# Chunk 0's first half: U by substitution over 32-token blocks in place of a 64-token inverse, and two query masks at an earlier place

## The chip, the cores and the metric

The kernel runs on 1 core of one Trainium2 chip. The time is device microseconds of one execution. Engines are called PE (TensorE), DVE (VectorE), ACT (ScalarE), POOL (GpSimd) and SP (SyncE, which here issues DMAs).

## The reference

```python
# batch B=4, heads H=8, sequence S=768, head size D=48
k_n = k / (norm(k) + 1e-6)
for t in range(S):
    y[:, :, t] = q[:, :, t] @ state
    v_old = state^T k_n[:, :, t]
    state = state + beta_t * outer(k_n[:, :, t], v_t - v_old)
x = y.transpose(0, 2, 1, 3).reshape(B * S, H * D)      # 3072 x 384
h = x @ w_in                                           # 384 -> 2048
out = (h * sigmoid(h)) @ w_out                         # 2048 -> 384
```

A recurrence over tokens (a delta rule) for each batch and head, followed by a feed-forward block over all tokens.

## The kernel before

The 768 tokens are cut into 6 chunks of 128, and each chunk into two halves of 64 (`hf`). The four batches form two groups `g` of two. In one half the update vectors U of all tokens follow from a triangular system: U = X (V - K S), with S the state at the start of the half and X the inverse of a 64x64 triangular matrix that is made of the score blocks (`aps[c, g][0]`), the key norms and beta. Chunk 0 begins with a zero state, so in its first half no term of the state enters.

For chunk 0, the scores are stored to memory and fetched back as blocks (`block_out`, `block_in`), `invert_first` inverts 16-token corners on DVE by rank-one steps, and then PE joins them in stages: `corner` and `straight` make the inverses of the four 32-token diagonal blocks of the partitions (into `xi`), `turned` makes a transposed copy of the even blocks, and `merge_half` (a first and a second product) fills in the 32x32 block between them, so that `xi` holds the 64-token inverse. Each stage is a generator over 16 heads-and-batches of one group `g`; it ends with copies out of PSUM by ACT and DVE. `joins(hf)` strings these stages together; between them single steps of the weights' narrowing are written in by hand (`fill`, `begin_next`). `narrow` takes a piece of 768 words per partition through two steps on ACT (L233, L234), two on DVE (L238, L242) and one on POOL (L246).

After the joins `masks` (L1364) multiplies the query scores of chunk 0 by a triangle, `solve(0)` runs `inner` (U = X V, L840; U goes to `zbuf` for the state and, for this first half, to `slab` for the outputs) and `first_outputs` (L884), which makes the transposed outputs `xT` of the first half; its last step is an add on DVE (L893). Then the first `hidden` product (L1046) can begin. The second half's joins (`joins(1)`) are laid between the first hidden products by the long script string: in it `s` is one step of `solve`, `f` one of `fill`, `q` the turning of one batch's queries, `j` one step of `joins(1)`, `b` is `begin_next`, `r` half a hidden product.

The order on each engine is written out: `pin` chains every operation behind the one before it on its engine. DMAs on SP's queue are in one line too. The later weight loads are paced: each is issued when a running count of PE's work (4 for a matmul, 2 for a transpose) reaches a number in `loads`. PSUM banks are handed out in turn from three rooms, `A` (3 banks), `CC` (3) and `M` (2). A matmul in fp32 appears as two PE instructions in the trace.

Of the kernel before, what the change touches and what calls it, by code (L numbers as in the profile page):

```python
# [13 lines left out]
ALU = mybir.AluOpType  # L14
# [5 lines left out]
def kernel(  # L20
# [10 lines left out]
    nc = tc.nc  # L31
    B, H, S, D = q.shape
    DM, DFF = moe_w_in.shape
    P = 128
# [5 lines left out]
    W = 64  # L40
# [622 lines left out]
    def invert_first(step):  # L663
# [77 lines left out]
        def straight(g, hf):  # L741

            pls = [bank(room, "pl") for room in (A, CC)]
            for i, n, k in heads(g, hf):
                for j in (2 * k + 1, 2 * k):
                    pin(nc.tensor.matmul(
                        pls[k][rows[j], T * i : T * (i + 1)], lhsT=y[rows[j], n, :],
                        rhs=up[rows[j], n, :], start=True, stop=True,
                    ))
                    yield  # L750
            for odd in (1, 0):
                for k, by in enumerate((by_act, by_dve)):
# [68 lines left out]
    def by_heads(t):  # L821
        return t[:, 0:DM].rearrange("p (u a d) -> p u a d", u=HB, a=NP)
# [12 lines left out]
    def inner(c, g, hf, room=CC):  # L835

        pz = bank(room, "pz")
        for u, p, e, n, _, _ in of_heads():
            rows = on(e, hf, g)
            yield pin(nc.tensor.matmul(  # L840
                pz[rows, n * D : (n + 1) * D], lhsT=xis[g][rows, u * H + 2 * p + e, :],
                rhs=vfs[c][rows, hf, g * HB + u, p, :], start=True, stop=True,
            ))
        to = zbuf[:, g * HB : (g + 1) * HB, hf, :, 0:D]
        if c == 0 and hf == 0:
            by = (by_act, by_dve) if g == 0 else (by_dve, by_act)
            at = slab[:, g * HB * NP * 2 * D + D :][:, 0 : HB * NP * 2 * D]
            by[0](at.rearrange("p (n w) -> p n w", w=2 * D)[:, :, 0:D], pz[:, 0:DM].rearrange("p (n d) -> p n d", d=D))
            by[1](to, by_heads(pz))
        else:  # L850
            by_act(to, by_heads(pz))

    def update(c, g, hf):

# [123 lines left out]
    def solve(c):  # L978

        if c == 0:  # L980
            together(inner(0, 0, 0, CC))
            together(inner(0, 1, 0, M))
            yield
            first_outputs(0)
            yield
            first_outputs(1)
            yield
            together(update(0, 0, 0), update(0, 1, 0))
            yield
# [12 lines left out]
            yield  # L1002
            return
        together(merge(c, 0, False), merge(c, 1, False))
        yield
        together(keys(c, 0, 0), keys(c, 1, 0))
        yield
        together(merge(c, 0, True), merge(c, 1, True))
        yield
        for hf in range(2):  # L1010
            if hf == 1:
                together(keys(c, 0, 1), keys(c, 1, 1))
                if c > 1:
# [12 lines left out]
            if hf == 0:  # L1026
                yield
# [286 lines left out]
    def first_queries(b):  # L1314
# [3 lines left out]

        score(0, b, (1,), (A, CC), evacuate)

    for b in range(2):
        turn(0, b, 1, M, b == 0)
    block_in(0)
# [18 lines left out]
    for b in range(2, B):  # L1342
# [19 lines left out]
    def masks(g, u):  # L1362
        to = aps[0, g][1][:, u]
        pin(nc.vector.tensor_tensor(  # L1364
            out=to, in0=to, in1=above[:].unsqueeze(1).to_broadcast([P, H, W]), op=ALU.mult
        ))

    for n in range(1 + Q):
        done = next(inv)
# [12 lines left out]
    pin(nc.gpsimd.memset(slab, 0.0))  # L1382

    def joins(hf, between=()):

        for stage in (
            corner(0, hf), corner(1, hf), turned(0, hf), turned(1, hf), straight(0, hf), merge_half(0, hf, False),
            straight(1, hf), merge_half(1, hf, False), merge_half(0, hf, True), merge_half(1, hf, True),
        ):
            yield from stage  # L1390
            for what in between[:1]:
                what()
            between = between[1:]

    def filled(n):
        return lambda: fill(n)

    def sized():
        size_half(0, pins[seen_on])
        begin_next()  # L1400

    def none():
        pass

    together(joins(0, [
        lambda: (size_half(0, pins[seen_on]), begin_next(),),
        lambda: (),
        lambda: (),
        lambda: (fill(1), fill(1),),
        lambda: (fill(1),),  # L1410
        lambda: (),
        lambda: (fill(1),),
        lambda: (fill(1), begin_next(),),
        lambda: (),
        lambda: (),
    ]))
    masks(0, 0)
    masks(0, 1)
    masks(1, 0)
    masks(1, 1)  # L1420

    pieces = chained(hidden(0, 0), hidden(0, 1), project())

# [146 lines left out]
                pieces = chained(feed_forward(1, 0), feed_forward(1, 1))  # L1570

    for text in (
        "s f3 s q q s j32 b j20 r f j8 q f j4 f j16 r j44 b j4 q j4 r f r j22 f j12 f j8 f b j8 f j4 r j20 e r f j99 h f r f2 l s l r l p r l f p l s l2 f r3 l3 p l s l4 p l2 s r l f l4 f l f l2 p l s l2 s p f r f r l r l2 g i p l p f i p f l i r2 i r v f i3 r3 i r i r i3 b r2 f2 r2 i r2 i2 r2 i f b i r i3 f2 r2 f r3 f i2 r f i f r3 f r f i f i2 r i r i k i2 b z r2 i r i r z r i r2 b r t s r b r f s r2 t s m r m t2 r b m f t m s f b r m2 b m f s r m r s m4 s m3 c m4 s r t G m r2 m4 V m s r m r m t2",
    ):
        script(text)
    for c in range(1, NCH):
# [62 lines left out]
```

## Time and profile before

| | us |
|---|---|
| timed runs, median (lowest to highest of 3) | 639.25 (639.19 to 642.03) |
| span of the profiled execution, first to last instruction | 636.1 |
| PE busy in it | 622.4 |
| DVE busy | 397.5 |
| ACT busy | 214.3 |
| first hidden product starts | 52.46 after the span's start |

For the profiled execution only the span is given; its own time, with what lies around the span, isn't. The median of the timed runs is 3.15 above the span. Times in the profile are microseconds from the first instruction. A row of the chain gives start, length and what ran; "issue" is time in which an engine waited for nothing that the profile shows. A row of stretches gives busy time and number of instructions of PE, weight loads, DVE, ACT and POOL, then the clock granted to PE (1.00 is full speed), the busy share of the DMA engines and GB/s. A row of a group gives line, engine, operation, output<-input, shapes and number, then busy time and mean ns of one, then the idle time before.

### The profile page before, as it was taken

How to read it: one execution, taken by the hardware profiler on the slowest of the kernel's cores; microseconds unless marked ns; L12 is line 12 of the kernel's file. 1: busy time of each engine (PE TensorE's matmuls, PEld its weight loads, DVE VectorE, ACT ScalarE, POOL GpSimd, SP SyncE). 2: the span in 40 equal slices, each digit the busy share in tenths (PEclk: the TensorE clock that was granted, in tenths of full speed). 3: DMA queues.
4: the chain of work that ended last, by engine and by line, in shares of the span. 5: the costliest groups of instructions: out<-in, count | busy, mean ns of one | idle time of the engine just before them, and what ended most of it. 6: DMA issues, size and time to landing. Idle time of an engine off the chain costs nothing.

```text
span 636.1 us, 21387 instructions
## 1 busy us (share of the span) xinstructions
PE 622.4 (98%) x9406; PEld 547.3 (86%) x9406; DVE 397.5 (62%) x910; ACT 214.3 (34%) x500; POOL 89.9 (14%) x92
## 2 busy tenths in 40 slices
PE   7979999999999999999999999999999999999997
PEld 5568788656799989989989989989989989989997
DVE  5786879999677974546974555975455964112112
ACT  3456673423351122451122451122451122441120
POOL 5033721345020020020020010020002000000000
PEclk9779999999999999999999999999999999999999
DMA  7966726350458460459151359232253133010101
GB/s 114 227 159 177 218 67 148 100 99 4 95 105 174 72 104 8 94 107 183 37 91 21 75 124 164 56 84 29 64 117 76 26 75 37 16 38 1 26 0 26
DMA packets 145676, 54.70 MB, mean 86 GB/s; under 512 B 117152, under 2 KB 138912, under 8 KB 145584
## 3 DMA queue, kind: packets, MB, share of 16 engines
q1 hardware_dynamic: 143136, 52.93, 40.5%
q8 instruction: 74, 1.21, 0.8%
q10 hardware_dynamic: 2448, 0.41, 0.4%
q14 instruction: 18, 0.15, 0.1%
HBM read 40.14 MB, written 11.01 MB: 80 GB/s over the span
## 4 chain that ended last, share of the span: by engine, by line
PE 94%; DVE 2%; DMA 1%; issue 1%; ACTq 0%; ACT 0%; POOL 0%; SPq 0%; DVEq 0%; POOLq 0%
PE phid L1046 40%; PE px L1163 17%; PE py L1163 13%; PE po L1090 5%; PE pb_c L840 3%; PE pa L529 2%; PE pb_c L828 2%; PE pyc L919 2%; PE pb_c L1090 2%; PE pb_c L860 2%; PE pyc L906 1%; PE px L782 1%; PE py L782 1%; PE pt L500 1%; DMA sums_of_w<-blocks 1%
## 5 line engine op out<-in xcount | busy, mean ns | idle before, releaser
L1046 PE MATMUL phid<-xT,w_in 128*128 128x256 f32 x1152 | 257.0, 381 | 0.2 <-DVE xT L893 0.2
L1046 PEld LDWEIGHTS phid<-xT,w_in 128*128 128x128 f32 x1152 | 216.4, 190 | 30.2 <-issue 0.9
L1056 ACT ACTIVATE gT<-phid 128x512 f32<-128x512 f32 x88 | 52.5, 597 | 144.8 <-PE phid L1046 140.5
L1144 DVE TENSOR_TENSOR sums_of_g<-gT 128x384 f32<-128x384 f32 (+1 forms) x60 | 30.4, 529 | 65.7 <-ACT gT L1056 55.4
L627 DVE SCALAR_TENSOR_TENSOR rank<-g,step,x 128x31 f32<-128x31 f32 (+15 forms) x124 | 49.8, 401 | 21.7 <-DMA g<-blocks 18.1
L1163 PE MATMUL px<-sums_of_w,sums_of_g 128*128 128x192 f32 x320 | 56.6, 329 | 0.0
L1163 PE MATMUL py<-w_out,sums_of_g 128*128 128x192 f32 x320 | 56.2, 328 | 0.0
L1163 PEld LDWEIGHTS py<-w_out,sums_of_g 128*128 128x128 f32 x320 | 52.3, 190 | 0.3
L1163 PEld LDWEIGHTS px<-sums_of_w,sums_of_g 128*128 128x128 f32 x320 | 52.2, 190 | 0.4
L632 DVE TENSOR_TENSOR x<-x,rank 128x31 f32<-128x31 f32 (+15 forms) x124 | 42.5, 342 | 4.3
L467 POOL TENSOR_TENSOR vf<-vf,n_slot 128x768 f32<-128x768 f32 x10 | 14.8, 1494 | 174.4 <-DMA vf<-in_v_dram 150.4
L544 ACT COPY xT<-pyc 48x128 f32<-48x128 f32 (+2 forms) x126 | 32.7, 260 | 1.7
L488 DVE STREAM_TRANSPOSE kq<-stage 128x512 f32<-128x512 f32 x28 | 28.4, 1115 | 5.2 <-DMA stage<-in_q_dram 5.2
L1163 PE MATMUL py<-w_out,gT 128*128 128x192 f32 x160 | 28.9, 330 | 0.0
L1174 DVE TENSOR_TENSOR o<-o,kept 128x192 f32<-128x192 f32 (+1 forms) x29 | 11.5, 422 | 26.7 <-ACT kept L1171 26.7
L1163 PE MATMUL px<-w_out,gT 128*128 128x192 f32 x160 | 27.9, 327 | 0.0
L1163 PE MATMUL px<-sums_of_w,gT 128*128 128x192 f32 x160 | 27.8, 327 | 0.0
L1163 PEld LDWEIGHTS px<-w_out,gT 128*128 128x128 f32 x160 | 26.5, 190 | 0.6
L550 POOL COPY g<-x 64x256 f32<-64x256 f32 x4 | 5.0, 1242 | 151.9 <-DVE x L635 151.9
L1163 PEld LDWEIGHTS py<-w_out,gT 128*128 128x128 f32 x160 | 26.1, 190 | 0.4
L865 DVE TENSOR_TENSOR state<-state,pb_c 128x384 f32<-128x384 f32 x22 | 11.2, 550 | 24.1 <-PE pb_c L860 24.1
L1163 PEld LDWEIGHTS px<-sums_of_w,gT 128*128 128x128 f32 x160 | 26.2, 190 | 0.1
(222 smaller groups left out, 931.2 us busy)
## 6 DMA issues: line engine op xcount, KB each, us to landing
vf<-in_v_dram SPq DMA_DIRECT2D x48, 96.0 KB, 2.8
out_dram<-o SPq DMA_DIRECT2D x42, 96.0 KB, 2.2
w_out<-in_moe_w_in_dram SPq DMA_DIRECT2D x4, 768.0 KB, 4.7
sums_of_w<-in_moe_w_out_dram SPq DMA_DIRECT2D x4, 768.0 KB, 4.1
blocks<-ap SPq DMA_DIRECT2D x44, 64.0 KB, 1.9
g<-blocks SPq DMA_DIRECT2D x5, 512.0 KB, 3.5
kb<-in_k_dram SPq DMA_DIRECT2D x12, 192.0 KB, 4.2
kb<-in_k_dram SPq DMA_DIRECT2D x24, 96.0 KB, 4.3
```

Source lines behind the costliest of these rows:

```text
L467: pin(nc.gpsimd.tensor_tensor(out=vf, in0=vf, in1=of, op=ALU.mult))
L488: pin(nc.vector.transpose(out=kqs[c, b][:, :, j, :].rearrange("p a (i m) -> p a m i", i=T), in_=src.rearrange("p a (m d) -> p a m d", d=D) ...
L529: pin(nc.tensor.matmul(pa[e][half, p * n * W : (p + 1) * n * W], lhsT=kq[rows, p, 0, half], rhs=kq[rows, p, js[0] : js[-1] + 1, half], sta ...
L544: return pin(nc.scalar.copy(to, of))
L627: pin(nc.vector.scalar_tensor_tensor(out=tv, in0=g[:, 0:m, m : m + 1].to_broadcast([P, m, n]), scalar=step[:, m : m + 1], in1=x[:, m : m + ...
L632: yield pin(nc.vector.tensor_tensor(out=x[:, 0:m, m:T], in0=x[:, 0:m, m:T], in1=tv, op=ALU.add))
L840: yield pin(nc.tensor.matmul(pz[rows, n * D : (n + 1) * D], lhsT=xis[g][rows, u * H + 2 * p + e, :], rhs=vfs[c][rows, hf, g * HB + u, p, : ...
L1046: pin(nc.tensor.matmul(ph[:, j * GT : (j + 1) * GT], lhsT=w_in[:, a, (2 * f + j) * P : (2 * f + j + 1) * P], rhs=xTs[c, hf][:, a, :], star ...
L1056: pin(nc.scalar.activation(out=hidden_of(c, hf, f), in_=ph[:], func=ACTF.Silu, scale=-0.5 if in_blocks(c) else 0.5))
L1090: pin(nc.tensor.matmul(pos[i][:, 0:DM], lhsT=hidden_of(0, hf, f // 2)[:, at : at + C], rhs=w_outs[f // HFF][:, f % HFF, :], start=(f == 0) ...
L1144: pin(nc.vector.tensor_tensor(out=sums_of_g[:, k, fs], in0=of[0], in1=of[1], op=op))
L1163: pin(nc.tensor.matmul(to, lhsT=at, rhs=quarter(f, *b) if isinstance(b, tuple) else sums_of_w[b][:, f], start=start and f == 0, stop=f == ...
```

## The change

For chunk 0's first half the 64-token inverse is no longer made. After `corner` and `straight`, `first_block` multiplies the even 32-token diagonal inverse with the values (U of the first 32 tokens), `across` multiplies the score block between the two with this U and adds it to the values of the odd block, and `last_block` multiplies the odd diagonal inverse with these. `turned`, both merges and `inner` are gone for this half; the second half of chunk 0 and all later chunks are as before. `last_block`'s result is copied to `slab` by ACT and, by `keep_last`, to `zbuf` by DVE. `straight` copies even blocks first in this half.

The scaling of the values (`size_half(0, ...)`, POOL) moves ahead of the clearing of `slab` (POOL). The masks of group 0 move to just behind that group's query scores, before the inversion; the masks of group 1 stand behind `across(1)`. Of the eight narrowing steps between `corner` and the second half's joins, five now come behind `first_outputs(1)` (`f5` in the script), where before three stood between `inner` and `first_outputs(0)` and none behind `first_outputs(1)`. Two paced loads (`fetch_w_out` 3 and 4) have numbers that are 128 lower, as much as the count falls short by the removed matmuls; the other numbers stay.

```diff
-            for odd in (1, 0):
+            for odd in ((0, 1) if hf == 0 else (1, 0)):
...
+    def first_block(g):
+        pz = both_blocks[g] = bank((CC, M)[g], "pz")
+        for u, p, e, n, _, _ in of_heads():
+            even, _ = blocks_of(e ^ g)
+            yield pin(nc.tensor.matmul(
+                pz[even, n * D : (n + 1) * D], lhsT=xis[g][even, u * H + 2 * p + e, 0:T],
+                rhs=vfs[0][even, 0, g * HB + u, p, :], start=True, stop=True,
+            ))
+        for k, by in enumerate((by_act, (by_dve, by_act)[g])):
+            even, _ = blocks_of(k)
+            by(zbuf[even, g * HB : (g + 1) * HB, 0, :, 0:D], by_heads(pz)[even])
+    def across(g):
+        pr = bank(CC, "pr")
+        ...
+                pr[odd, n * D : (n + 1) * D], lhsT=aps[0, g][0][even, u, 2 * p + e, T:W],
+                rhs=zbuf[even, g * HB + u, 0, p, 0:D], start=True, stop=True,
+        ...
+            pin(nc.vector.tensor_tensor(out=to, in0=to, in1=by_heads(pr)[odd], op=ALU.add))
+    def last_block(g):
+        ...
+                pz[odd, n * D : (n + 1) * D], lhsT=xis[g][odd, u * H + 2 * p + e, T:W],
+                rhs=vfs[0][odd, 0, g * HB + u, p, :], start=True, stop=True,
+        ...
+        by_act(at.rearrange("p (n w) -> p n w", w=2 * D)[:, :, 0:D], pz[:, 0:DM].rearrange("p (n d) -> p n d", d=D))
...
         if c == 0:
-            together(inner(0, 0, 0, CC))
-            together(inner(0, 1, 0, M))
-            yield
             first_outputs(0)
...
     first_queries(1)
+    masks(0, 0)
+    masks(0, 1)
     step = block_steps(0)
...
-        (WINDOW + PACKET * 15 + 45, fetch_w_out, 3),
-        (WINDOW + PACKET * 15 + 60, fetch_w_out, 4),
+        (WINDOW + PACKET * 14 + 173, fetch_w_out, 3),
+        (WINDOW + PACKET * 14 + 188, fetch_w_out, 4),
...
     corner, turned, straight = next(inv)
+    size_half(0, pins[seen_on])
     pin(nc.gpsimd.memset(slab, 0.0))
...
-    together(joins(0, [ ... ]))          # with size_half, begin_next and 5 fill steps between the stages
-    masks(0, 0)
-    masks(0, 1)
-    masks(1, 0)
-    masks(1, 1)
+    for stage, then in (
+        (corner(0, 0), lambda: begin_next()),
+        (corner(1, 0), lambda: fill(2)),
+        (straight(0, 0), None),
+        (straight(1, 0), None),
+        (first_block(0), lambda: fill(1)),
+        (first_block(1), lambda: begin_next()),
+        (across(0), None),
+        (across(1), lambda: (masks(1, 0), masks(1, 1))),
+        (last_block(0), lambda: keep_last(0)),
+        (last_block(1), lambda: keep_last(1)),
+    ):
+        together(stage)
+        if then is not None:
+            then()
...
-        "s f3 s q q s j32 b j20 r ...
+        "s q q s f5 j32 b j20 r ...
```

More of the change, by code (lines that the diff above doesn't have):

```diff
@@ L833, in keys, with inner @@
         pin(nc.vector.tensor_tensor(out=to, in0=to, in1=by_heads(ph), op=ALU.add))
-    def inner(c, g, hf, room=CC):
-        pz = bank(room, "pz")
+    def inner(c, g, hf):
+        pz = bank(CC, "pz")
         for u, p, e, n, _, _ in of_heads():
@@ L844, in inner, with blocks_of @@
         to = zbuf[:, g * HB : (g + 1) * HB, hf, :, 0:D]
[L845 to L851, printed above, removed]
+        by_act(to, by_heads(pz))
+    def blocks_of(k):
+        return slice(W * k, W * k + T), slice(W * k + T, W * (k + 1))
+    both_blocks = {}
+    def first_block(g):
[11 more added lines that the diff above has]
+        pr = bank(CC, "pr")
+        for u, p, e, n, _, _ in of_heads():
+            even, odd = blocks_of(e ^ g)
+            yield pin(nc.tensor.matmul(
+                pr[odd, n * D : (n + 1) * D], lhsT=aps[0, g][0][even, u, 2 * p + e, T:W],
+                rhs=zbuf[even, g * HB + u, 0, p, 0:D], start=True, stop=True,
+            ))
+        for k in range(2):
+            _, odd = blocks_of(k)
+            to = vfs[0][odd, 0, g * HB : (g + 1) * HB]
+            pin(nc.vector.tensor_tensor(out=to, in0=to, in1=by_heads(pr)[odd], op=ALU.add))
+    def last_block(g):
+        pz = both_blocks[g]
+        for u, p, e, n, _, _ in of_heads():
+            even, odd = blocks_of(e ^ g)
+            yield pin(nc.tensor.matmul(
+                pz[odd, n * D : (n + 1) * D], lhsT=xis[g][odd, u * H + 2 * p + e, T:W],
+                rhs=vfs[0][odd, 0, g * HB + u, p, :], start=True, stop=True,
+            ))
+        at = slab[:, g * HB * NP * 2 * D + D :][:, 0 : HB * NP * 2 * D]
+        by_act(at.rearrange("p (n w) -> p n w", w=2 * D)[:, :, 0:D], pz[:, 0:DM].rearrange("p (n d) -> p n d", d=D))
     def update(c, g, hf):
@@ L1319, in first_queries, with masks @@
         score(0, b, (1,), (A, CC), evacuate)
+    def masks(g, u):
+        to = aps[0, g][1][:, u]
+        pin(nc.vector.tensor_tensor(
+            out=to, in0=to, in1=above[:].unsqueeze(1).to_broadcast([P, H, W]), op=ALU.mult
+        ))
     for b in range(2):
@@ L1381, with joins @@
     corner, turned, straight = next(inv)
+    size_half(0, pins[seen_on])
     pin(nc.gpsimd.memset(slab, 0.0))
-    def joins(hf, between=()):
+    def joins(hf):
         for stage in (
@@ L1390, in joins, with keep_last @@
             yield from stage
[L1391 to L1416, printed above, removed]
-    masks(0, 0)
-    masks(0, 1)
-    masks(1, 0)
-    masks(1, 1)
+    def keep_last(g):
+        by_dve(zbuf[:, g * HB : (g + 1) * HB, 0, :, 0:D], by_heads(both_blocks.pop(g)))
+    for stage, then in (
[13 more added lines that the diff above has]
+            then()
     pieces = chained(hidden(0, 0), hidden(0, 1), project())
```

7 lines of the change are left out of this document (1 added, 6 removed).

## The prediction

> **What bounds the kernel now.** I read the core's span and the summary of engines and DMA queues first, then the chain of work that ended last, then the granted clock in short stretches, and last the DVE, ACT and POOL work around the change.
>
> ```profile
> core 0: 636.1 us, clock 0.986
> ```
> ```profile
> PE 622.4 (98%) x9406; PEld 547.3 (86%) x9406; DVE 397.5 (62%) x910; ACT 214.3 (34%) x500; POOL 89.9 (14%) x92
> ...
> q8 instruction: 74, 1.21, 0.8%
> ```
>
> PE is the bound: of the 636.1 us it idles 13.7. The change lies in the first 52 us, where chunk 0 is solved before the first hidden product can start. From then on the order of PE work is unchanged, so the edit is worth what it moves the first hidden product, plus what it costs just behind it. That is seen in the chain:
>
> ```profile
> 38.09 1.05 issue
> ...
> 41.62 1.35 issue
> ...
> 43.93 0.91 PE pb_c L806 x17
> 44.83 1.88 PE pb_c L840 x32
> 46.71 1.60 PE pz L840 x30
> 48.31 0.07 PE py L884 x2
> 48.41 0.89 PE py L884 x44
> 49.30 1.02 PE pt L500 x8
> 50.33 0.94 PE py L884 x46
> 51.27 0.47 ACT xT L544
> 51.76 0.57 DVE xT L893
> 52.33 0.14 issue
> 52.46 1.53 PE phid L1046 x6
> ...
> 54.83 0.13 PE pl L717 x2
> ```
>
> The columns are start, length and what ran. From 42.97 (41.62 + 1.35) to 51.27 PE works without a gap: the second merges (L806), `inner` (L840), `first_outputs` (L884), two turns. Then comes a fixed tail to the first hidden product at 52.46: 1.19 us of evacuation. Ahead of it PE stands twice with the cause "issue". I read these two as PE waiting for its own instructions: 2 x 9406 instructions in 74 fetches of the instruction queue are 254 each, 127 weight loads and 127 matmuls, and the stretch 38.45:41.86 below, which holds the work between the two stands, has exactly x127.
>
> ```profile
> 19.00:22.00 3.00, 2.55 (x14) 1.72 (x13) 0.04 (x1) 1.26 (x7) 0.00 (x0) 0.90 0.86 256
> 38.00:39.00 1.00, 0.09 (x11) 0.00 (x0) 0.97 (x2) 0.73 (x2) 0.37 (x1) 0.72 0.73 215
> 48.00:49.00 1.00, 1.00 (x50) 1.00 (x52) 0.87 (x2) 0.00 (x0) 0.00 (x0) 0.66 0.06 16
> ```
> ```profile
> 35.03:38.45 3.42, 2.39 (x137) 1.99 (x132) 2.94 (x8) 1.25 (x4) 2.85 (x2) 1.00 0.47 89
> 38.45:41.86 3.41, 2.48 (x127) 2.35 (x128) 3.29 (x7) 1.60 (x6) 0.91 (x1) 0.50 0.64 215
> 41.86:45.27 3.41, 2.30 (x72) 2.24 (x73) 2.23 (x5) 2.78 (x5) 0.92 (x1) 0.50 0.79 254
> 45.27:48.69 3.42, 3.42 (x82) 3.42 (x82) 3.23 (x7) 0.48 (x2) 0.00 (x0) 0.50 0.47 87
> ```
>
> The columns are stretch, its length, busy time of PE, weight loads, DVE, ACT, POOL, then the granted clock (last but two). A clock of 0.72 over 38:39 is full speed until 38.44 and half after it; 0.66 over 48:49 puts the return at 48.68. So the chain from 38.44 to 48.68, the very part that is rewritten, runs at half clock. [...]
>
> **The change part by part.** Of a product, 16 matmuls make 32 PE instructions per batch group. Removed for the first half: `turned` (2 x 32), four merges (4 x 32), `inner` (2 x 32): 256. Added: `first_block`, `across`, `last_block`, 2 x 32 each: 192, of 32x32 blocks with 48 columns. `corner` and `straight` stay, `straight` now directly behind `corner`.
>
> *PE price of an added product.* At half clock the merges (32x32 blocks, 32 columns) take 0.91/17 for two, 26.8 ns each; with 48 columns in place of 32 that makes 40 ns, 1.29 us per 32, and 0.65 at full clock. The bounds are 26.8 ns (0.86 us) and `inner`'s 1.88/32 = 58.8 ns (1.88 us); I take 40 as the shape is the merges'. Six products are 7.7 us.
>
> *Where they start.* The instructions behind the first stand begin at the third instruction after `corner` (128), `turned` (64) and `straight`'s first group (64): the x137 of the stretch up to 38.45 are 6 left of `corner`, these 128, and 3. After the change the same count is reached with `corner`, both `straight`, and two of `first_block`. I keep the same arrival, 39.14 (38.09 + 1.05). The next 127 instructions are used up after 5.1 us, later than the 3.83 us between the two arrivals, so the second stand (1.35) goes.
>
> *What feeds them.* `first_block` needs the scaled values and the diagonal blocks.
>
> ```profile
> 35.52 1.42 POOL L1382 MEMSET sums_of_w<- 128x1584 f32 x1 [3.56 <-DVE sums_of_w L694]
> 36.90 1.47 POOL L457 TENSOR_TENSOR vf<-vf,n_slot 128x768 f32<-128x768 f32 x1
> ```
>
> These two POOL steps swap, so the values are ready near 37.0 instead of 38.4 and the slab is cleared by 38.4, long before it is filled. On DVE the narrowing step L238 still stands ahead of the diagonal copies:
>
> ```profile
> L547 DVE COPY xi<-pb_c 32x256 f32<-32x256 f32 x6 | 2.5, 424 | 1.2 <-PE pb_c L806 1.1
> L1364 DVE TENSOR_TENSOR ap<-ap,above 128x512 f32<-128x512 f32 x4 | 2.5, 686 | 0.0
> L238 DVE TENSOR_SCALAR w_in<-w_in 128x768 uint32<-128x768 uint32 x3 | 2.4, 810 | 0.1
> L242 DVE SCALAR_TENSOR_TENSOR w_in<-raw,w_in 128x768 uint32<-128x768 uint32 x2 | 1.9, 954 | 0.0
> L893 DVE TENSOR_TENSOR xT<-xT,py 128x384 f32<-128x384 f32 x2 | 1.1, 548 | 0.7 <-ACT xT L544 0.7
> ...
> L724 DVE SCALAR_TENSOR_TENSOR sums_of_w<-pl,second,pick 64x128 f32<-64x128 f32 x1 | 0.3, 335 | 0.0
> ```
>
> After four corner copies from about 35.3 (0.34 each) it ends near 37.7 and the first even block is copied by 38.1, before 39.14. Inside the chain each product of one group has the other group's 1.29 us to be evacuated in: `first_block` by a copy of 0.56 at most, then L242's 0.95, `across` by two adds of 0.55. These fit to within 0.1 us. At half clock I therefore let PE run through: 39.14 + 7.7 = 46.9, against 48.31 before.
>
> *The rest of the chain* is `first_outputs` 0.94, turns 1.02, `first_outputs` 0.94, 2.9 us at full clock. With the clock back at 48.68, 1.8 us at half make 0.9 of it; 2.0 remain, PE ends at 50.7 and the hidden product starts at 51.9: 0.6 earlier. [...] I take 0.9.
>
> *The two early masks* (2 x 0.69) go where DVE does 0.04 us of work in 19:22 while the score blocks are fetched: nothing, and without that hole 1.4. Before, all four masks lay under `inner` on PE and cost nothing, so nothing is gained by it either; two still stand ahead of the last z copies, which `update` needs much later.
>
> *The fills moved* from inside the solve to behind `first_outputs` put L238, L242, L238 (0.69 + 0.95 + 0.69 by their undisturbed lengths, 2.3 us) ahead of the second half's corner copies (2 x 0.35) on DVE. PE wants these 2.4 us after the hidden start (54.83 - 52.46); they come after 2.9. PE waits 0.5 there; I take 0.4, since that place already lost a little.
>
> *The loads* are paced by PE's count, which is now 64 instructions short, so all but the two that were shifted come 64 instructions later. The tightest is the last `w_in` piece:
>
> ```profile
> 63.27 0.37 SPq L292 DMA_DIRECT2D sums_of_g<-in_moe_w_in_dram  x1
> ```
> ```profile
> 69.87 0.89 ACT L233 ACTIVATE w_in<-sums_of_g 128x768 f32<-128x768 f32 x1
> ```
> ```profile
> sums_of_g<-in_moe_w_out_dram SPq DMA_DIRECT2D x2, 768.0 KB, 4.9
> ```
>
> Landing takes 4.9 us, so 1.7 us are spare; 64 instructions are 0.8 us of small matmuls or several of hidden ones. ACT, with the hidden evacuations behind it, could wait 0 to 1 us. I take 0, as small ones fill that stretch.
>
> **Sum.** 0.9 - 0.4 = 0.5 us. The timed median, 639.25, is 3.15 above the profiled span, which I take as what lies around it: 635.6 + 3.15 = 638.7 us. A measurement of this kernel tells about 0.5% (3.2 us) from no change, so this counts as the same.
>
> **The rivals.** *Full clock through the solve.* With six products at 0.65 only the evacuations and the instructions' arrival hold: `last_block` starts at 42.97, `first_outputs` at 44.3, the hidden product at 48.4, 4.0 earlier, 3.5 net: 635.8 us. If the clock returns only at 45.27, because PE has no stand in 41.86:45.27 any more, it is 50.3, and 637.6. For it: the two stands that emptied those stretches shrink to one. Against: 2.48 us of busy 32x32 work in 3.41 did not raise the clock. [...]
>
> [...]
>
> *It does nothing*, the solve being hidden: excluded as the chain runs through it; I give it no chance of its own beside the forecast, whose size is as small.
>
> **How the numbers follow.** Forecast, clock as before: 0.46, 638 to 639.5. Full clock earlier: 0.30, of which 0.22 under 636.05. Clock later: 0.24, of which 0.14 above 642.45 (two windows and the load, or three). So faster 0.22, same 0.64, slower 0.14. The range takes the full-clock case in whole and the slow one to its second window: 635.6 to 642.2.
>
> **What would show it.** Right: first hidden product near 51.5; one stand by "issue" near 38 to 39 and none at 42; products of 32 in 1.3 us; a short PE wait at L733 for DVE's L724 some 3 us behind the hidden start. Wrong: granted clock at 1.00 in 39:45 (first rival), 0.50 past 49 (second), products at 1.9 us, or ACT waiting for `sums_of_g` near 70.

## The result and the profile after

| | before | after |
|---|---|---|
| timed runs, median (lowest to highest of 4 each), us | 639.63 (639.19 to 642.03) | 654.18 (654.09 to 657.21) |
| ratio, with its 95% interval | | 1.0234 (1.0211 to 1.0257) |
| span of the profiled execution, us | 636.1 | 655.5 |
| PE busy in it, us | 622.4 | 629.2 |
| first hidden product starts, us | 52.46 | 54.25 |

The changed kernel is slower by 14.5 us. The forecast was 638.7 in a range of 635.6 to 642.2. The profiled execution of after took 657.21, 3.0 above its median (the spans of its other executions are 652.4 to 652.5), so the steps below are a little longer than those of a typical execution.

The engines and queues of the page of after:

```profile
PE 629.2 (96%) x9342; PEld 552.6 (84%) x9342; DVE 402.0 (61%) x909; ACT 213.4 (33%) x497; POOL 90.1 (14%) x92
...
q8 instruction: 73, 1.20, 0.8%
```

PE has 64 matmuls less to do than before, and yet is busy for 6.8 us more (629.2 against 622.4) and idle for 26.3 instead of 13.7. I read the first as half clock (the mean granted clock is 0.977 against 0.986) and the second as waiting. The waits of PE in after (what ran, what it waited for, then us in all, times, longest):

```profile
PE pt L500 <- DMA sums_of_g<-in_q_dram: 3.6, 2, 2.5
PE px L782 <- issue: 2.5, 2, 1.4
...
PE pb_c L828 <- issue: 2.0, 1, 2.0
PE pb_c L858 <- DVE xi L547: 1.4, 1, 1.4
```

Two of these lie in the solve (L858, and L500, the turning of chunk 1's queries). The other two, L782 (at 351 and 554 us) and L828 (at 444 us), are code that the change doesn't touch. The chain of waits around the solve, as start, length and what ran (the "issue" of 0.80 is a wait for DVE, which is busy with the narrowing step L238 until 38.25):

```profile
37.48 0.80 issue
...
38.83 1.41 PE pb_c L858 x29
...
41.60 2.40 PE pb_c L871 x57
...
46.04 3.37 DMA sums_of_g<-in_q_dram
...
49.54 1.94 PE pt L500 x8
...
53.25 5.15 DMA sums_of_g<-in_q_dram
```

The first hidden product runs beside the second of these transfers and is not on the chain:

```profile
54.25 1.53 PE L1082 MATMUL phid<-xT,w_in 128*128 128x256 f32 x6
```

The chain that in the kernel before ran through PE from 42.97 now leaves PE twice, each time for a query load of chunk 1 (L144). Their issues in SP's queue, before and then after (start, length, line and number):

```profile
43.53 7.10 SPq L144 DMA_DIRECT2D sums_of_g<-in_q_dram  x6
```
```profile
44.96 8.92 SPq L144 DMA_DIRECT2D sums_of_g<-in_q_dram  x6
```

The six issues begin 1.43 us later and end 3.25 later (53.88 against 50.63). The clock of after, in rows of stretches as before:

```profile
32.80:36.22 3.42, 2.34 (x196) 2.05 (x198) 3.29 (x7) 1.86 (x3) 1.35 (x1) 1.00 0.66 115
36.22:39.63 3.41, 2.00 (x86) 1.81 (x88) 3.30 (x4) 1.45 (x4) 1.48 (x2) 0.50 0.72 228
...
43.04:46.45 3.41, 3.41 (x86) 3.22 (x84) 3.21 (x6) 1.70 (x3) 1.35 (x1) 0.50 0.66 219
46.45:49.87 3.42, 2.36 (x64) 2.08 (x61) 1.96 (x4) 1.12 (x3) 0.00 (x0) 0.50 0.56 104
49.87:53.28 3.41, 3.41 (x84) 2.96 (x86) 0.00 (x0) 1.44 (x3) 0.00 (x0) 0.50 0.02 6
53.28:56.70 3.42, 2.66 (x114) 2.05 (x106) 3.10 (x6) 1.94 (x3) 0.87 (x1) 1.00 0.89 185
56.70:60.11 3.41, 1.58 (x46) 1.38 (x47) 3.12 (x6) 0.60 (x1) 2.46 (x2) 1.00 0.45 165
```

Half clock holds from 36.22 to 53.28, 17.1 us against the 10.2 around the solve before, and again from 60.11. It halved behind rows in which PE was busy for 2.34 and for 1.58 us of 3.4. A row of this length, 3.41 us, is called a window below.

To see where the other time goes, I took the start of the same step, the SiLU of each hidden product on ACT, in both traces. One such pair, before and then after:

```profile
472.16 0.60 ACT L1056 ACTIVATE gT<-phid 128x512 f32<-128x512 f32 x1 [2.13 <-PE phid L1046]
```
```profile
490.02 0.60 ACT L1092 ACTIVATE gT<-phid 128x512 f32<-128x512 f32 x1 [2.13 <-PE phid L1082]
```

That is a lag of 17.86 us (490.02 - 472.16). Worked out in the same way for six of the 96 products, and for every kernel of the study, the lags against the kernel before are these. The heads of the columns are the times of the step in the kernel before.

| kernel | 57.05 | 115.18 | 276.42 | 371.98 | 476.86 | 614.59 |
|---|---|---|---|---|---|---|
| after | 5.40 | 6.98 | 8.98 | 12.49 | 17.85 | 19.36 |
| e1_loads | 5.57 | 5.89 | 7.69 | 9.59 | 12.35 | 14.35 |
| e2_loads_pad | 4.82 | 8.21 | 8.73 | 8.73 | 9.97 | 11.04 |
| e4_before_pad | 9.08 | 9.85 | 12.06 | 15.29 | 21.14 | 22.95 |
| e6_before_pad2 | 5.08 | 5.40 | 5.39 | 5.66 | 5.91 | 6.18 |
| e5_before_late | 4.16 | 5.17 | 4.91 | 5.03 | 6.89 | 7.38 |
| e7_early_q | 1.61 | 4.20 | 5.95 | 7.40 | 11.49 | 13.45 |
| e8_early_q_pad | 2.60 | 5.86 | 5.53 | 5.53 | 6.83 | 7.41 |
| e9_early_q_pad_fill | 5.19 | 6.37 | 6.63 | 6.63 | 6.89 | 7.54 |
| e10_pad_late | 3.32 | 8.22 | 7.68 | 8.49 | 9.74 | 9.79 |
| e11_q_pad_warm | 1.62 | 8.77 | 8.44 | 8.59 | 9.62 | 9.79 |
| e12_pad_late_masks | 6.56 | 10.21 | 10.29 | 10.29 | 11.05 | 11.45 |
| e13_q_pad_fills | 1.67 | 3.58 | 4.10 | 4.69 | 5.58 | 6.94 |
| e14_pad_behind_straight | 4.62 | 5.61 | 5.62 | 5.66 | 6.14 | 6.06 |
| e15_pad_straight_fill | 4.46 | 4.57 | 4.93 | 4.94 | 5.20 | 5.84 |

Each row is one execution, and all are set against one execution of before with a short span (636.1; other executions of it have 636.2 to 641.3). So the level of a row can be off by two or three us against the medians: after and e10 run the same instructions up to 57 us, and stand at 5.40 and 3.32 there. The last column of after is 19.36 where the medians differ by 14.5, so its rises are too long as well. What I read from a row is where it rises.

In after only 5.4 us are there behind the solve; 12.4 us (19.36 - 6.98) come in steps after 115 us, in work that the edit left as it was. One of these steps, in stretches, before and then after:

```profile
446.00:448.00 2.00, 2.00 (x101) 1.93 (x91) 1.02 (x2) 0.63 (x2) 0.00 (x0) 1.00 0.03 8
```
```profile
444.00:446.00 2.00, 0.44 (x18) 0.32 (x19) 1.76 (x5) 1.16 (x2) 0.00 (x0) 0.95 1.00 116
446.00:448.00 2.00, 1.54 (x47) 1.45 (x46) 1.20 (x2) 0.00 (x0) 0.00 (x0) 0.50 0.06 12
448.00:450.00 2.00, 2.00 (x7) 2.00 (x8) 1.02 (x2) 0.00 (x0) 0.00 (x0) 0.50 0.00 0
```

In the kernel before PE is busy throughout that stretch at full clock. In after it stands for 2 us in the middle of the small products L828 (this is the "issue" wait of 2.0 above), and then runs at half clock, large products too.

### The profile page after: what moved, and what is told of

Same layout as the page of the kernel before. It is cut to its first block, busy times and chain, and to the rows that moved or that the text cites. A ratio compares the mean times of both kernels' runs of the same rounds, so it can differ in the third digit from the quotient of the medians.

```text
span 655.5 us, 21252 instructions
## 1 busy us (share of the span) xinstructions
PE 629.2 (96%) x9342; PEld 552.6 (84%) x9342; DVE 402.0 (61%) x909; ACT 213.4 (33%) x497; POOL 90.1 (14%) x92
## 4 chain that ended last, share of the span: by engine, by line
PE 90%; DMA 4%; DVE 2%; issue 2%; ACT 1%; SPq 1%; ACTq 0%; DVEq 0%
PE phid L1082 37%; PE px L1199 17%; PE py L1199 12%; PE po L1126 5%; PE pb_c L840 2%; PE pa L529 2%; PE pb_c L828 2%; PE pyc L958 2%; PE pb_c L1126 2%; PE pb_c L899 1%; DMA sums_of_g<-in_q_dram 1%; PE pyc L945 1%; DMA kb<-in_k_dram 1%; PE px L782 1%; PE pt L500 1%
## 5 line engine op out<-in xcount | busy, mean ns | idle before, releaser
L1199 PE MATMUL px<-sums_of_w,sums_of_g 128*128 128x192 f32 x320 | 58.0, 333 | 0.9 <-issue 0.9
L632 DVE TENSOR_TENSOR x<-x,rank 128x31 f32<-128x31 f32 (+15 forms) x124 | 42.5, 343 | 4.3
L1199 PE MATMUL px<-sums_of_w,gT 128*128 128x192 f32 x160 | 30.2, 346 | 0.0
L1199 PEld LDWEIGHTS px<-sums_of_w,gT 128*128 128x128 f32 x160 | 28.5, 204 | 0.1
```

The source lines that it names most:

```text
L632: yield pin(nc.vector.tensor_tensor(out=x[:, 0:m, m:T], in0=x[:, 0:m, m:T], in1=tv, op=ALU.add))
L1199: pin(nc.tensor.matmul(to, lhsT=at, rhs=quarter(f, *b) if isinstance(b, tuple) else sums_of_w[b][:, f], start=start and f == 0, stop=f == ...
```

## The experiments

After the result I held two theories for the late steps. **T1, the place of the fetches**: PE's instructions come in pieces of some 254 matmuls and weight loads (2 x 9406 in the 74 packets of the instruction queue). The edit takes out 128 instructions, 64 matmuls with their weight loads, which is half a piece. In every dense run of small products behind it PE then comes to the end of a piece at another place, waits there by "issue", and the clock falls. **T2, the paced loads**: the loads that are issued by PE's count come 64 instructions late, PE waits for data, and one delay makes the next.

An "empty product" below is a 32x32 matmul of the identity with 16 columns whose result nobody reads. 32 of them are 64 matmuls in the trace and 128 instructions, and they aren't counted for the pacing of the loads unless the text says so.

### e1_loads, e2_loads_pad: the count put right, then the instructions too

```diff
-        (first_block(1), lambda: begin_next()),
+        (first_block(1), lambda: (begin_next(), counted(128))),   # begun[0] += 128
-        (WINDOW + PACKET * 14 + 173, fetch_w_out, 3),             # and fetch_w_out 4
+        (WINDOW + PACKET * 15 + 45, fetch_w_out, 3),
```

e2 has this and 32 empty products behind `first_outputs(1)` (`x32` in the script).

> The changed kernel with PE's count raised by 128 behind the second first_block product, and the two shifted loads at their old numbers, so that every paced load stands at the same step of the program as in the kernel before; no instruction of PE is added. Theory 'late loads' (the query loads of chunk 1 come late because the count is 128 short, and that is the whole loss): about 639 us. Theory 'instruction pieces' (PE has 128 instructions fewer, half of one fetch, so in all later chunks the dense bursts of small products meet the ends of the fetches elsewhere and PE waits there; the late loads are only the first 7.4 us of the lag): 646 to 649 us, first hidden product near 51 to 54, but the steps of the lag near 250, 350, 450 and 550 us stay. Theory 'clock' (products on two row groups keep the clock low): PE works without a gap up to the first hidden product, yet at half clock past 49 us, 653 us.

> As e1_loads, and 32 empty 32x32 products with 16 columns (64 matmuls, 64 weight loads, not counted for the loads) behind first_outputs(1), so that PE has as many instructions again as in the kernel before; their result is read by nobody. Theory 'instruction pieces': the later steps go, 639 to 641 us. Theory 'late loads': e1_loads plus about 0.8 us for the empty products. A theory 'banks' (the rotation of the PSUM room CC is one bank off behind the change, and that makes the later waits): no better than e1_loads, 647 us or more.

Measured: e1 653.17 us, ratio 1.0189 (1.0156 to 1.0223); e2 646.76, ratio 1.0095 (1.0061 to 1.0128); before on the same chip 640.55. The loads at their old place in the program bring 1 us by the medians and 2.9 by the ratios (1.0234 against 1.0189), and the intervals of the two overlap, so their worth is not settled here. The 32 empty products, which are only work, bring another 6.4. In the table e1 rises by 8.5 us after 115 us, e2 by 2.8. Putting the count right at this place did not free the query turn: PE still waits 1.5 us there for the load in e1. The clock theory had 653 us for e1, and half clock did hold until 60.21 in its trace; but PE did not work without a gap (it also waits 2.4 us for `xi`), and the later steps stayed. e2 missed the 639 to 641 of the pieces theory and is near the 647 of the banks theory: 8.21 of its 11.04 us of lag are there at 115 us, ahead of the late steps.

### e4_before_pad, e6_before_pad2: half a piece and a whole piece in the kernel before

```diff
-        "s f3 s q q s j32 b j20 ...",
+        "s f3 s q q s x32 j32 b j20 ...",      # e4: 32 empty products; e6: x64
```

> The kernel before with the same 32 empty products behind first_outputs(1) (128 more PE instructions, half a fetch), not counted for the loads; nothing else. Theory 'instruction pieces': 8 to 12 us slower than the kernel before, 648 to 652 us, with waits of PE by 'issue' in the bursts of chunks 2 to 5. Theories 'late loads' and 'banks': only the price of the products, 640.4 us.

> The kernel before with 64 empty products (256 more PE instructions, a whole fetch) at the same place. Theory 'instruction pieces': the bursts meet the fetches as in the kernel before again, so only the price of the products, 640.5 to 642 us, below e4_before_pad. If it were the products themselves that cost, twice the loss of e4_before_pad.

Measured: e4 657.23, ratio 1.0233 (1.0185 to 1.0281); e6 646.36, ratio 1.0079 (1.0052 to 1.0106). Nothing else in the kernel before was changed. Half a piece costs 16.7 us by the medians (the four executions of e4 lie between 651.97 and 660.82, so the size is rough), and twice as much empty work costs 5.8. Both are more than was expected. Their places in the table say the same more sharply: e4 rises by 13.1 us after 115 us, in the same columns as after, and e6 by 0.8. What e6 loses is nearly all there at 57 us (5.08), right behind the empty products, where PE stands by "issue" for 2.0 us at L717. Two of PE's waits in e4:

```profile
PE pb_c L828 <- issue: 3.0, 1, 3.0
...
PE px L782 <- issue: 2.2, 2, 1.2
```

These are lines on which after waits too. The stretches of e4, and one of e6, around the same products:

```profile
446.00:448.00 2.00, 1.36 (x128) 1.25 (x114) 1.86 (x10) 0.96 (x2) 0.00 (x0) 1.00 1.54 134
448.00:450.00 2.00, 0.00 (x0) 0.00 (x0) 1.85 (x5) 0.19 (x1) 0.00 (x0) 0.61 0.45 64
450.00:452.00 2.00, 1.69 (x48) 1.59 (x48) 0.46 (x2) 0.00 (x0) 0.00 (x0) 0.50 0.03 8
```
```profile
448.00:450.00 2.00, 2.00 (x117) 1.93 (x108) 0.95 (x3) 0.73 (x2) 0.00 (x0) 1.00 0.04 8
```

In e4 PE does nothing from 448 to 450 and comes back at half clock; in e6, late by 6 us but shifted by a whole piece, it has no gap. In these two runs, then, it is the place within the piece that makes the late steps (13.1 against 0.8 us), and not a delay as such.

### e5_before_late, e7_early_q: the query loads

e5 is the kernel before with the count lowered by 128, so that its loads come as late as in after while PE's own instructions stay (the last two numbers are lowered as in after). e7 is after with both query loads of chunk 1 paced far earlier.

```diff
-        lambda: (),
+        lambda: (counted(-128),),                                 # e5, behind the start of the merges
```
```diff
+        (WINDOW + PACKET * 2 + 30, load_q, 1, slice(HB * 0, HB * 0 + HB)),      # e7
+        (WINDOW + PACKET * 2 + 60, load_q, 1, slice(HB * 1, HB * 1 + HB)),
-        (WINDOW + PACKET * 4 + 15, load_q, 1, slice(HB * 0, HB * 0 + HB)),
-        (WINDOW + PACKET * 5 + 0, load_q, 1, slice(HB * 1, HB * 1 + HB)),
```

> The kernel before, PE's instructions untouched, with the count lowered by 128 behind the first merge of the joins (so the loads paced after it come 64 instructions late, the last two shifted back as in the change). If the queries' lateness is what costs early, the second and third query turns wait and the first hidden products lag by 1 to 5 us, 641 to 645 us, with no later steps. If the kernel before had room there: 640.5 us.

> The changed kernel, PE's instructions untouched, with both query loads of chunk 1 right behind the third w_in piece (ahead of the fourth), at counts 30 and 60 in place of packets 4 and 5. Two causes are now held: late query loads make the lag at the first hidden products (5.4 to 7 us), and the place of the fetches in PE's instructions makes the steps behind 200 us (12.4 us in the changed kernel's profile, 13.1 in the kernel before with 32 empty products). If so: no wait of the query turns, first hidden product near 52, the later steps of 8 to 12 us stay, 646 to 650 us. If the early lag is not the queries but half clock: first hidden product past 54, about 652 us.

Measured: e5 646.3, ratio 1.0082 (1.006 to 1.0104); e7 652.39, ratio 1.0177 (1.0134 to 1.022); before on the same chip 640.2. The wait of e5 is the one of after, at the same line:

```profile
PE pt L500 <- DMA sums_of_g<-in_q_dram: 3.1, 2, 2.0
```

So late loads alone cost the kernel before some 6 us; PE's wait for the query loads is 3.1 of them in the trace, and the weight loads came later too. e7 takes the query loads' lateness from the changed kernel: PE no longer waits for them, and the lag at 57 us falls from 5.40 to 1.61. But its row still rises by 9.3 us after 115 us, and the median falls by 1.8 only (3.6 by the ratios; the intervals of after and e7 overlap a little). T2 is true for the first 57 us and does not explain what comes behind. The two numbers of e7's other theory came true as well, a first hidden product past 54 (54.04) and 652 us: half clock holds for 17.1 us in e7 too (33.67 to 50.73), and with no wait for queries left, it, the wait for `xi` (1.7) and PE's stands are what remains to make the first hidden product 1.6 us late.

### e8_early_q_pad, e9_early_q_pad_fill: both cures, the empty products ahead of the solve

e8 is e7 with e1's count and 32 empty products ahead of `corner`; e9 also moves two narrowing steps from behind `corner(1)` to behind `straight(1)`.

```diff
-        (corner(1, 0), lambda: fill(2)),
+        (corner(1, 0), None),                                     # e9
-        (straight(1, 0), None),
+        (straight(1, 0), lambda: fill(2)),
```

> As e7_early_q, with 32 empty products ahead of the first corner product, where PE waits 0.7 us for DVE (so that PE has as many instructions as in the kernel before from there on), and PE's count raised by 128 behind the second first_block product with the two shifted loads at their old numbers. With the two causes: both go, 638 to 641 us. If the place of the empty products matters for more than the number of instructions (they move the ends of the fetches in the solve of chunk 0 by half a fetch): a wait by 'issue' there of up to 4 us and 641 to 644 us.

> As e8_early_q_pad, with the two fill steps behind corner moved behind straight on DVE, so that the diagonal blocks are copied before L238, which took 2.09 us in the changed kernel while POOL worked. If that wait set the start of first_block (38.8 us there): 1 us faster than e8_early_q_pad. If PE's instructions or the clock set it: the same.

Measured: e8 645.31, ratio 1.0077 (1.0056 to 1.0098); e9 645.16, ratio 1.0077 (1.0058 to 1.0095). The late steps are nearly gone (1.6 and 1.2 us after 115 us). Both are above the 638 to 641 of "both go" and above the 644 that the other case allowed for. In neither does PE wait for `xi` any more (in e8 the empty products and a stand keep it from the products until `xi` is there), and the move of the narrowing steps brings nothing in the time: in both kernels PE waits by "issue" within the solve, for 1.6 and 1.4 us in e8, at L746 and L871, and for 1.8 and 1.9 in e9.

### e10_pad_late, e12_pad_late_masks: only the place of the fetches, and the masks

e10 is after with nothing but 32 empty products near 100 us, behind the whole solve. e12 is e10 with the two early masks back behind `across(1)`.

```diff
-        "... g i p l p f i p f l i r2 i r v ...",
+        "... g i p l p f i p f l i r2 x32 i r v ...",
```
```diff
-    masks(0, 0)
-    masks(0, 1)
-        (across(1), lambda: (masks(1, 0), masks(1, 1))),
+        (across(1), lambda: (masks(0, 0), masks(0, 1), masks(1, 0), masks(1, 1))),      # e12
```

> The changed kernel with only 32 empty products in the run of hidden products near 100 us (not counted for the loads), so that from there on PE has as many instructions as in the kernel before; the late query loads stay. Two causes (late queries early, place of the fetches late): the lag up to 95 us stays at 6 to 7 us, the steps of 12.4 us behind 200 us shrink to 0 to 3, 646 to 649 us. If what makes the later steps is not the place of the fetches but the changed PSUM rotation or the loads: 654 us.

> As e10_pad_late with the two masks of group 0 back behind across(1). Predicted price of the early masks: nothing either way; so the time of e10_pad_late to within 1 us. If the two masks behind across hold up the last copies of U (0.7 us each ahead of the copies to zbuf): up to 1.4 us slower.

Measured: e10 645.48, ratio 1.0092 (1.0059 to 1.0124); e12 645.94, ratio 1.0106 (1.0073 to 1.014); before on the same chip 640.36. The code of the solve is that of after; PE still waits there for the query loads (2.0 us) and runs at half clock. The kernel is 8.7 us faster than after all the same, with more work. The same stretches of e10:

```profile
444.00:446.00 2.00, 2.00 (x15) 2.00 (x14) 0.09 (x1) 0.43 (x1) 0.00 (x0) 1.00 0.04 8
446.00:448.00 2.00, 1.71 (x131) 1.37 (x129) 0.00 (x0) 0.33 (x1) 0.00 (x0) 1.00 0.00 0
```

The clock stays at 1.00, and of 2 us of standing 0.3 are left in these rows. This is the largest part of the loss. The rotation of the PSUM banks in room CC, the other theory, is that of after in e10, so it isn't what makes the late steps. e12 shows nothing for the masks: the intervals of the two lie over each other.

### e11_q_pad_warm, e13_q_pad_fills: what is left in the solve

e11 is e7 with 29 empty products near 100 us and three wide ones (128 rows, 384 columns) in the solve, to hold the clock up. e13 is e10 with e7's early query loads and three of the five narrowing steps taken ahead of `first_outputs(0)`, as they stood before.

```diff
-        (straight(1, 0), None),
+        (straight(1, 0), lambda: warm(2)),                        # e11; one more behind corner(1)
```
```diff
-        "s q q s f5 j32 b j20 ...",
+        "f3 s q q s f2 j32 b j20 ...",                            # e13
```

> As e7_early_q with the empty products near 100 us (29 of them), and three products of full 128 rows and 384 columns (uncounted, read by nobody) where PE waits in the solve of chunk 0: one behind corner(1), two behind straight(1). If half clock (17.1 us in e7_early_q, 10.2 in the kernel before) is a third cause, the clock stays at full speed for a window or more longer between 33 and 51 us and the first hidden product comes 1.5 to 4 us earlier than in e7_early_q: 639 to 643 us. If PE waits for instructions anyway: the clock changes, the time doesn't, 643 to 646 us.

> As e10_pad_late, with the query loads early (as e7_early_q) and three of the five fill steps back ahead of first_outputs(0) (script: f3 s q q s f2). Both causes removed at their places: the lag at the first hidden products 0 to 1.5 us (1.6 in e7_early_q), some 2 us more up to 95 us from the fetches there, later steps 0 to 3: 641 to 645 us. If the fills behind first_outputs were what delayed the second half's joins: 1 us less lag at 57 us than e7_early_q; if not, 1.6 again.

Measured: e11 645.99, ratio 1.0089 (1.0058 to 1.012); e13 643.35, ratio 1.006 (1.0037 to 1.0083). In e11 the clock did hold until 44.6:

```profile
42.00:44.60 2.60, 1.88 (x72) 1.58 (x66) 2.37 (x4) 2.33 (x5) 0.78 (x1) 1.00 1.25 139
```

The time did not follow: PE stood by "issue" for 2.3 us at one of the wide products, and the first step's lag, 1.62, is that of e7, 1.61. The run adds three wide products to PE's work, so it doesn't price the clock alone. e13 has the lowest median of the changed kernels; its chain in the solve:

```profile
39.23 1.41 PE pb_c L858 x29
...
44.62 0.43 issue
...
47.82 1.49 PE py L923 x48
...
52.69 1.17 issue
...
54.17 1.49 PE phid L1082 x6
```

The first hidden product starts 1.7 us later than in the kernel before. The six products end at 47.82, 0.5 ahead of the 48.31 at which `first_outputs` began before. From there to the hidden product it is 6.35 us against 4.15, with half clock until 50.38 and the new stand of 1.17.

### e14_pad_behind_straight, e15_pad_straight_fill: every instruction behind the solve's start at its old place

e14 is e13 with the empty products directly behind `straight(1)` and not near 100 us, and with e1's count. e15 also moves two narrowing steps there, as e9 did.

```diff
-        (straight(1, 0), None),
+        (straight(1, 0), lambda: pad()),                          # e15: (fill(2), pad())
```

> Early query loads and three fills ahead of first_outputs(0) as in e13_q_pad_fills, but the 32 empty products stand right behind straight(1) (not near 100 us), and PE's count is raised by 128 behind the second first_block product with the two shifted loads at their old numbers: from first_block on PE has as many instructions as in the kernel before, and from across on every load but the queries stands where it stood. If the rest of 3 us is the place of the fetches between 39 and 100 us: lag at 105 us 0 to 1.5 us, 639.5 to 642 us. If it is the new solve: the same 3 us or more, 643 to 645 us.

> As e14_pad_behind_straight with the two fill steps behind corner moved behind straight, so that DVE copies the diagonal blocks ahead of L238. PE is busy with empty products or waits for instructions there, so: within 0.7 us of e14_pad_behind_straight. If L238 (2 us with POOL at work) holds first_block: 1 us faster, and then the fastest of the changed kernels, 638.5 to 640 us.

Measured: e14 643.91, ratio 1.0061 (1.0034 to 1.0087); e15 643.42, ratio 1.0056 (1.0039 to 1.0073); before on the same chip 640.0. Their rows in the table are nearly flat from the first column on (e15: 4.46 to 5.84). Nearly all that is left of the loss lies ahead of the first hidden product. The chain of e15:

```profile
37.72 1.75 issue
39.46 0.99 PE pad L1441 x45
...
43.11 2.12 issue
45.23 2.52 PE pb_c L871 x29
...
50.77 1.49 PE py L923 x48
52.26 1.90 PE pt L500 x8
54.16 1.57 PE py L923 x46
...
56.92 1.10 PE phid L1082 x4
```

Both stands of the kernel before are back, at 37.72 and 43.11, as soon as the number of instructions is the old one, with products of `across` and `last_block` still to go behind the second. From its end to `first_outputs` it is 5.54 us (45.23 to 50.77); in the kernel before it was 5.34 (42.97 to 48.31). From `first_outputs` to the hidden product it is 6.15 against 4.15, as these rows run at half clock until 55.65. So the 4.46 us by which the first hidden product is late are 2.26 at the end of the second stand, 0.20 in the products and 2.00 behind them. No kernel of the study beats the kernel before.

## Why the prediction was wrong, point by point

**The step that failed** is the sentence "From then on the order of PE work is unchanged, so the edit is worth what it moves the first hidden product, plus what it costs just behind it." The order is unchanged, but PE's stands come a whole number of pieces of some 254 instructions apart, as the counts below show, and the edit takes out 128, half a piece, so every later piece ends at another place in the work. The prediction had worked out this very size, 254 instructions, and used it for the solve alone. e10 puts a price on it: 8.7 of the 14.5 us (654.18 against 645.48, not run side by side; by the ratios it is 9.1). e4 shows it without the edit, +16.7 us, and e6 shows that a whole piece brings no late steps. The traces fit stands that are waits for the fetch of such a piece. Here are the stand of after at L828, the instruction queue's packets in the stretch 443.50:443.60 (packets, MB, share of the time of 16 engines), and the stretches between this stand and the one ahead of it, in after and then in e4:

```profile
446.46 0.36 PE L828 MATMUL pb_c<-state,kq 48*64 48x48 f32 x5 [2.02 <-issue]
```
```profile
q8 instruction: 1, 0.02, 90.9%
```
```profile
352.48:446.46 93.98, 91.96 (x1272) 84.59 (x1273) 62.71 (x147) 28.70 (x74) 8.69 (x9) 0.98 0.52 90
```
```profile
355.28:450.31 95.03, 92.08 (x1272) 84.67 (x1273) 62.94 (x148) 28.73 (x74) 8.68 (x9) 0.97 0.50 89
```

One packet of 16 KB (1.20 MB in 73) starts there and takes 1.45 us (0.909 x 16 x 0.1), so it lands near 445.0, and PE goes on 1.4 us later. From the stand ahead PE has run 2545 instructions (1272 + 1273), ten pieces of 254.5, in both kernels. In the traces of all 16 kernels PE has 59 stands by "issue" of more than 0.4 us behind 36 us. Each of them ends 1.2 to 1.8 us behind the landing of such a packet (1.55 and 1.26 for the two around the solve of before, 1.43 for the one above), and each comes 193 or 194 instructions behind a multiple of 256, if the instructions of PE's sequencer are counted in.

**The paced loads** were the second. I priced the tightest weight piece at 0 and did not look at the query loads of chunk 1, which hang on the same count. e5 puts 6 us on late loads in the kernel before, e7 gives 1.8 us of median (654.18 to 652.39) back in the changed kernel. Whether the price of the fetches and that of the loads add up was not tried. Nor did the tightest weight piece come in time: ACT waits 2.16 us for it in after, where it starts on it at 77.81 and not at 69.87 as before. No run tells what that costs.

```profile
77.81 0.91 ACT L233 ACTIVATE w_in<-sums_of_g 128x768 f32<-128x768 f32 x1 [2.16 <-DMA sums_of_g<-in_moe_w_in_dram]
```

**The clock** came back later than the 48.68 of the forecast, at 53.28. The chances have this as "clock later", 0.24, and the range reaches up to 642.2 for it; no run shows what decides when the clock comes back, so those two were my estimate. In the row 43.04:46.45 above the new products kept PE busy for 3.41 of 3.41 us and the granted clock was 0.50, and it was 0.50 in the two rows behind it too; PE's wait for the queries falls into the first of these, where it was busy for 2.36 of 3.42. The clock is the smaller part of the loss: e7 has half clock for as long (17.1 us), without those waits, and its first step is 1.61 us late. The faster rival, full clock, did not come. Of the 0.9 in the sum the chain gives 0.6; no run shows a source for the other 0.3, and the first hidden product came 1.79 us later (54.25 against 52.46).

**The price of a product** was nearly right. I took 40 ns; the chain of after has 1.41/29 = 49 and 2.40/57 = 42. In e13, where no query load stands between, six products take 39.23 to 47.82 with a stand of 0.43 in them, 42.5 ns each (8.16/192).

**The start** at 39.14 came out (38.83 in after, 39.23 in e13) by luck, for another reason: PE waited 1.4 us for DVE's `xi`. The prediction had the narrowing step L238 end near 37.7. It ended at 38.25, as the DVE and then the POOL timeline of after show:

```profile
36.16 2.09 DVE L238 TENSOR_SCALAR w_in<-w_in 128x768 uint32<-128x768 uint32 x1
38.28 1.79 DVE L547 COPY xi<-pb_c 32x256 f32<-32x256 f32 x4
```
```profile
36.28 1.42 POOL L1421 MEMSET sums_of_w<- 128x1584 f32 x1
```

Against a mean of 0.81 in the kernel before, the step took 2.09 beside the clearing of the slab, which stands next to it since POOL's two steps were swapped. In e15, where it stands behind `straight(1)`, it took 0.69:

```profile
38.81 0.69 DVE L238 TENSOR_SCALAR w_in<-w_in 128x768 uint32<-128x768 uint32 x1
```

What this move is worth in the whole is less than the runs can tell (e9 against e8, e15 against e14).

**The second "issue" stand** is gone in after, as predicted, but that was worth nothing: in e13 stands of 0.43 and 1.17 come later, and in e15 it is back, at 43.11. By the counts above (193 or 194 behind a multiple of 256 for all 59) the stands go with the number of instructions, and not with the place in the code.

**The masks** show no cost, as predicted (e12). **The fills** moved behind `first_outputs`, which I priced at 0.4, weren't tried alone, and PE's wait for L724 that was to show them is not among its waits in after (e8, e9 and e11 have 0.4 us of it); e13, which moves three back and takes the query loads early, is 2.1 us below e10.

**What stays open**: the last 3 to 4 us (e13, e14 and e15 against before). They lie in the solve and just behind it. The forecast had the six products end at 46.9 and the hidden product 5.0 later; in e13 they end at 47.82 and it is 6.35. Part of that is half clock in `first_outputs` and the turns, as in e15, and part is stands. The clock was held up for a part of the solve in e11, and the wait for `xi` was gone in e9, e14 and e15; each time PE stood by "issue" within the solve (2.3, 1.9, 2.1 and 2.1 us at the longest). That the arrival of the instructions holds the solve, so that fewer products in it save next to nothing, fits all of these; no run made the instructions come sooner, so it is not shown.

## What to carry to other kernels

Before an edit that adds or removes PE instructions early in a program, divide PE's instructions by the number of instruction fetches, and see whether the shift is a part of such a piece: where dense small products come later, they can gain or lose more than the edit itself (here a shift of 128 of some 254 lost 16.7 us in e4, and its repair gained 8.7 in e10). Test a change of this sort with as many empty products as bring the shift to a whole piece, put behind the changed place. And where transfers are paced by a count of work, follow every entry of the list behind the edit, not only the one with the least room.

## What was not expected of the hardware

- Work that nobody needs made the kernel 8.7 us faster (e10), and the same work made the kernel before 16.7 us slower (e4).
- Around the long stands the DMA engines were loaded: a share of 1.00 in 444:446 of after, 1.54 in 446:448 of e4, against 0.03 in the kernel before in 446:448. The packet that PE waited for in after took 1.45 us, where the mean of the 73 is about 1.15 (0.8% of 16 x 655.5 us, over 73); whether the load had a part in that was not tried.
- In after the clock fell behind a window in which PE was busy for 2.34 of 3.42 us, and did not rise behind one in which it was busy for 3.41 of 3.41 with blocks of 32 rows (43.04:46.45).
- Every stand of PE by "issue" of more than 0.4 us behind 36 us, 59 in 16 traces, ended 1.2 to 1.8 us behind the landing of a 16 KB packet of the instruction queue.
- One DVE step over 128x768 words took 2.09 us beside POOL's clearing and 0.69 behind it (after, e15).
